# An expert's fixed number of rows: 608 instead of 640

## The chip, the cores and the metric

The kernel runs on one core of one Trainium2 chip. The metric is the device time of one execution in microseconds (us); three runs of the kernel before gave 948.78, 949.24 and 949.30, median 949.24. The engines: PE is TensorE's matmul, PEld its weight load, DVE VectorE, ACT ScalarE, POOL GpSimd (which also issues the indirect DMAs), SP SyncE (which issues the plain DMAs).

## The reference, cut to what matters

Attention within chunks of 64 gives 2304 tokens of 512 numbers; a dense layer with 2048 hidden units follows; then each token goes to two of eight experts, and the experts' weighted results are added up:

```python
def _moe2_ref(x, w_gate, w_noise, noise, w1, w2):     # x: 2304 x 512, after the dense layer
    logits = x @ w_gate
    noise_scale = np.log1p(np.exp(x @ w_noise))
    noisy_logits = logits + noise_scale * noise
    top2 = np.argpartition(-noisy_logits, 2, axis=1)[:, :2]
    ...                                               # top2_w: softmax over the two
    for e in range(E):                                # 8 experts
        for k in range(2):
            mask = top2[:, k] == e
            h = np.maximum(x[mask] @ w1[e], 0.0)      # 512 -> 1024
            out[mask] += top2_w[mask, k, None] * (h @ w2[e])   # 1024 -> 512
```

With two experts for each of 2304 tokens an expert has 576 rows on average. How many it really has is known on the chip only.

## The kernel before, in words

**Numbers.** Every f32 operand of the large products is split into a high part, rounded to the matmul's short f32 form (float32r), and a low part, the rest. A product is then three MATMULs (`PASSES`): high by high, high by low, low by high. The small products (attention, gate) are left in plain f32.

**Stages.** Five blocks of 4, 3, 4, 4 and 3 tiles of 128 tokens go through attention and the dense layer; the gate's results of each block are turned into places in a table in DRAM (`gate_ps`): each expert has a region of 2688 rows, and a token's row number and weight are scattered to the next free place of its two experts. Then come nine groups (`groups`): expert 0 in two parts (its first three tiles, and the two tiles up to `CAP`), experts 1 to 6 whole with five tiles each, and expert 7 again in two parts of three and two tiles. A part or an expert takes the first `CAP` = 640 places of its region, whether filled or not; unfilled places point at rows of zeros in DRAM. If an expert has more than `CAP` rows, `overflow` handles the rest after everything else.

**A group.** `exp_slots` or `exp_slots_q` fetches the places (`tab`, and for the second form `tq`, from which `exp_index` makes indices). The rows are fetched by indirect DMAs from GpSimd: `exp_gather` one per tile of 128 rows (for the second part of expert 0 and for expert 1), `exp_gather_q` four per tile, each for 32 rows cut into quarters (for all others). They are transposed on TensorE (`exp_tr`) or, the quarters, on VectorE (`exp_tr_q`, `quarters_t`), and ScalarE and VectorE write the high and the low part into Xa or Xe (Xb for the first group), which the groups use in turn.

Then the group runs over 8 units (`U2`) of 128 hidden numbers each. For a unit, `exp_h` makes the first products (L284): per half of the rows, 12 MATMULs (4 pieces of the 512 by 3 passes) with the unit's weights stationary and the rows as moving columns; with 640 rows that is two halves of 320, with 256 or 384 rows one of that width. ScalarE (L585) and VectorE (L586) take the result out of PSUM as the unit's high and low g. One unit later `exp_o` makes the second products (L293): for each tile, three MATMULs with the tile's 128 columns of g stationary and 512 columns of weights moving, all 8 units added up in PSUM. `exp_y` scales each tile's sum by the rows' weights (L612, L614; the very last tile in two halves, L609 and L610) and adds it to the output with an indirect DMA from GpSimd (L615).

**Order.** The order of work on TensorE, VectorE and ScalarE is written out by hand (`manual_schedule`); the loop at the end of `tile_kernel` puts the next group's gathers and transposes and the weights' splitting (`pump`: L128, L129) behind each unit. GpSimd's and SP's queues are ordered by a planner from its own estimates. A group's rows are asked for one group ahead: the first three tiles in units 3, 5 and 6 of the group before the last, the others early in the group before.

Of the kernel before, what the change touches and what calls it, by code (L numbers as in the profile page):

```python
# [8 lines left out]
F32 = mybir.dt.float32  # L9
# [4 lines left out]
AF = mybir.ActivationFunctionType  # L14
ALU = mybir.AluOpType
# [4 lines left out]
P = 128  # L20
NT = 2304
DM = 512
KD = DM // P
# [6 lines left out]
XO = [("a", 0), ("b", 0), ("a", 0), ("b", 0), ("a", 0)]  # L30
NB = len(BT)
GRP = list(zip(B0, BT))
CAP = 640
CT = CAP // P
EARLY = 384
RB = 21
RGN = RB * P
# [5 lines left out]
def tile_kernel(ctx, tc, qkv, w1u, w2u, wg, noise, out):  # L43
    nc = tc.nc
# [43 lines left out]
    cnt = const.tile([P, NE + 1], I32, name="cnt")  # L88
# [4 lines left out]
    arena = const.tile([P, 7, DM], F32, name="arena")  # L93
    X = {"a": const.tile([P, 8 * CAP], F32R, name="Xa")}
    late = tc.tile_pool(name="late", bufs=1)
# [4 lines left out]
    def xview(where, n):  # L100
        a, off = where
        return X[a][:, off:off + 8 * n].rearrange("p (j k n) -> p j k n", j=2, k=KD)

    xb = [xview(XO[b], BT[b] * P) for b in range(NB)]
    st = {}
# [183 lines left out]

    def s2(acc, g, w, tiles, first, last):  # L290
        for i in range(tiles):
            for j, (a, b) in enumerate(PASSES):
                nc.tensor.matmul(acc[i], g[:, a, i * P:(i + 1) * P], w[:, b, DM:],  # L293
                                 start=(first and j == 0), stop=(last and j == 2))
            tick()

# [7 lines left out]
    def gtile():  # L304
        return work.tile([P, 2 * CAP], F32R, tag="g", bufs=2, name="g")

# [49 lines left out]

    def quarters_t(dst, src):
        nc.vector.transpose(dst.rearrange("p (c b j) -> p c b j", c=KD, b=KD),  # L360
                            src.rearrange("p (c i b) -> p c b i", c=KD, b=KD))

    def gate_l(t):
        st.pop(("x2", t))
# [151 lines left out]
    def exp_slots(key, e, t0, nt, off):  # L516
        tab = work.tile([P, CT, 2], I32, tag="tab", bufs=4, name="tab")
        r0 = e * RGN + t0 * P
        nc.sync.dma_start(tab[:, :nt], table[r0:r0 + nt * P, :].rearrange("(t p) c -> p t c", p=P))
        st["tab", key] = tab  # L520
        st["xg", key] = xview(off, nt * P)


    def exp_slots_q(key, e, t0, nt, off):
# [14 lines left out]

    def exp_gather_q(key, i):  # L540
        xr = work.tile([P, DM], F32, tag="x2", bufs=3, name="xrq")
        for c in range(KD):
            nc.gpsimd.indirect_dma_start(  # L543
                out=xr[:, c * P:(c + 1) * P], out_offset=None, in_=x2q,
                in_offset=bass.IndirectOffsetOnAxis(ap=st["iq", key][:, i * KD + c:i * KD + c + 1], axis=0))
        st["xr", key, i] = xr

    def exp_tr_q(key, i):
        x = st["xg", key]
        xt = arena[:, 5 + i % 2]  # L550
        quarters_t(xt, st.pop(("xr", key, i)))
        xt = xt.rearrange("p (c b j) -> p b c j", c=KD, b=KD)
        hi, lo = (x[:, j, :, i * P:(i + 1) * P].rearrange("p b (c j) -> p b c j", c=KD) for j in range(2))
        nc.scalar.activation(hi, xt, AF.Copy)
        nc.vector.tensor_tensor(lo, xt, hi.bitcast(F32), op=ALU.subtract)

# [7 lines left out]
    def exp_tr(key, i):  # L564
        xr = st.pop(("xr", key, i))
        x = st["xg", key]
        pt = bank(("p7", "p6")[i % 2], [P, KD, P], "ptg")
        for kd, xc in enumerate(blocks_of(xr)):
            nc.tensor.transpose(pt[:, kd, :], xc, ident)  # L569
        hi, lo = (x[:, j, :, i * P:(i + 1) * P] for j in range(2))  # L570
        nc.scalar.activation(hi, pt, AF.Copy)
        nc.vector.tensor_tensor(lo, pt, hi.bitcast(F32), op=ALU.subtract)

    def exp_h(key, e, u, nt):
        x, w = st["xg", key], st["w", e, u]
        g = gtile()[:, :2 * nt * P].rearrange("p (j n) -> p j n", j=2)
        st["g", key, u] = g
        if nt * P <= 512:
            parts = [(0, nt * P)]
        else:  # L580
            parts = [(0, nt * P // 2), (nt * P // 2, nt * P // 2)]
        for t0, n in parts:
            h = hbank(n)
            s1(h, w, x, t0, n)
            nc.scalar.activation(g[:, 0, t0:t0 + n], h, AF.Relu)  # L585
            nc.vector.scalar_tensor_tensor(g[:, 1, t0:t0 + n], h, 0.0, g[:, 0, t0:t0 + n].bitcast(F32),  # L586
                                           op0=ALU.max, op1=ALU.subtract)

    def exp_last(key, e, nt):
        for i in range(nt):  # L590
            for u in (U2 - 2, U2 - 1):
                g, w = st["g", key, u], st["w", e, u]
                for j, (a, b) in enumerate(PASSES):
                    nc.tensor.matmul(st["acc", key][i], g[:, a, i * P:(i + 1) * P], w[:, b, DM:],  # L594
                                     start=False, stop=(u == U2 - 1 and j == 2))

    def exp_o(key, e, u, nt):
# [3 lines left out]

    def exp_y(key, e, nt):
        tab = st.pop(("tab", key))
        for i in range(nt):
            y = arena[:, i]
            sc = tab[:, i, 1:2].bitcast(F32)
            if key == (NE - 1, 1) and i == nt - 1:
                h = DM // 2
                nc.vector.tensor_scalar(y[:, :h], st["acc", key][i][:, :h], sc, None, op0=ALU.mult)  # L609
                nc.scalar.activation(y[:, h:], st["acc", key][i][:, h:], AF.Copy, scale=sc)  # L610
            elif i % 2 == 0:
                nc.vector.tensor_scalar(y, st["acc", key][i], sc, None, op0=ALU.mult)  # L612
            else:
                nc.scalar.activation(y, st["acc", key][i], AF.Copy, scale=sc)  # L614
            s = nc.gpsimd.indirect_dma_start(  # L615
                out=out, out_offset=bass.IndirectOffsetOnAxis(ap=tab[:, i, 0:1], axis=0),
                in_=y, in_offset=None, compute_op=ALU.add)
            for o in st.setdefault(("out_st", e), []):
                tc.declare_no_dep(s.ins, o.ins, reason="an expert has a token once")
            st["out_st", e].append(s)  # L620
# [11 lines left out]

    def overflow():
        for e in range(NE):
            n = nc.values_load(cnt[0:1, e:e + 1], min_val=0, max_val=RGN)
            with tc.For_i(CAP, n, P) as i:
                tab = work.tile([P, CT, 2], I32, tag="tab", bufs=4, name="tabo")
                nc.sync.dma_start(tab[:, 0], table[bass.ds(i + e * RGN, P), :])
                xr = work.tile([P, DM], F32, tag="x2", bufs=3, name="xo")
                nc.gpsimd.indirect_dma_start(out=xr, out_offset=None, in_=x2d,  # L640
                                             in_offset=bass.IndirectOffsetOnAxis(ap=tab[:, 0, 0:1], axis=0))
                pt = bank("p7", [P, KD, P], "pto")
                for kd, xc in enumerate(blocks_of(xr)):
                    nc.tensor.transpose(pt[:, kd, :], xc, ident)
                xt = arena[:, 5].rearrange("p (h k) -> p h k", h=KD)
                nc.scalar.activation(xt, pt, AF.Copy)
                acc = bank("p0", [P, DM], "acco")
                for u in range(U2):
                    raw = work.tile([P, 2 * DM], F32, tag="raw", bufs=3, name="rawo")
                    nc.sync.dma_start(raw, w2u[e * U2 + u])  # L650
                    h = bank(HB[u % 2], [P, P], "ho")
                    for kd in range(KD):
                        nc.tensor.matmul(h, raw[:, kd * P:(kd + 1) * P], xt[:, kd], start=(kd == 0), stop=(kd == KD - 1))
                    g = work.tile([P, DM], F32, tag="r", bufs=2, name="go")
# [4 lines left out]
                    out=out, out_offset=bass.IndirectOffsetOnAxis(ap=tab[:, 0, 0:1], axis=0),  # L659
# [289 lines left out]
    for i in range(3):  # L949
        at(side, EU + i, exp_tr, (0, 0), i)  # L950
# [131 lines left out]
```

## Time and profile before

| what | value |
|---|---|
| median of three runs | 949.24 us |
| span of the profiled execution | 947.0 us (the page shows no time of its own beyond the span) |
| PE busy | 921.0 us, 97% |
| DVE, ACT, POOL busy | 489.1, 336.3, 242.0 us |
| granted TensorE clock | 0.996 on the mean |
| first products with 320 columns (L284) | 576 on Xe, 576 on Xa |
| first products with 256 columns | 192 |
| quarter gathers (L543) | 120 |
| scatters to the output (L615) | 40 |

Matmuls are pipelined: the duration shown for one (310 ns for 320 columns) begins while the one before still runs, so the time that one product costs is read from the distance between starts, or from the chain of waits, which counts each only from the end of the one before. The granted clock is a share of 2.4 GHz.

### The profile page before, as it was taken

The numbers are of one execution on the slowest core, as the hardware profiler recorded it, in microseconds if no ns is written. First come the engines' busy times: TensorE is split into PE (matmuls) and PEld (weight loads), VectorE is DVE, ScalarE is ACT, GpSimd is POOL, SyncE is SP. The second block draws the span as 40 slices with busy tenths as digits, with TensorE's granted clock in tenths as the row PEclk, the third lists the DMA queues.
The fourth block names the chain that finished last, engine by engine and source line by source line (L and its number), as shares of the span: only waits on it lengthen the run. The fifth ranks groups of instructions, "written<-read, shape, count | busy, mean of one in ns | idle before, by whom it ended". The sixth has DMA issues, their size and how long they took to land. (4 is left out here: it accounts for less than half of the span.)

```text
span 947.0 us, 14446 instructions
## 1 busy us (share of the span) xinstructions
PE 921.0 (97%) x5814; PEld 780.9 (82%) x5814; DVE 489.1 (52%) x912; ACT 336.3 (36%) x644; POOL 242.0 (26%) x219
## 2 busy tenths in 40 slices
PE   6999999999999999999999999999999999999995
PEld 3677788887777777888988899989899899898894
DVE  7999954544453444456642555445545544441311
ACT  4555433332233222245531533333333333321210
POOL 0000000030002000213105166745736454432311
PEclk9999999999999999999999999999999999999998
DMA  9636549122112410025533663644636354140421
GB/s 342 207 99 204 175 146 343 35 68 68 34 34 57 134 35 1 1 90 91 188 101 67 169 155 107 146 119 101 143 113 143 115 122 129 51 59 20 56 33 27
DMA packets 50364, 102.41 MB, mean 108 GB/s; under 512 B 17136, under 2 KB 23152, under 8 KB 50288
## 3 DMA queue, kind: packets, MB, share of 16 engines
q1 hardware_dynamic: 38736, 80.38, 27.3%
q0 software_dynamic: 11552, 21.02, 12.0%
q8 instruction: 47, 0.77, 0.3%
q14 instruction: 29, 0.24, 0.1%
HBM read 78.05 MB, written 23.28 MB: 107 GB/s over the span
## 5 line engine op out<-in xcount | busy, mean ns | idle before, releaser
L293 PE MATMUL bp<-w,g 128*128 128x512 f32 x1812 | 455.1, 397 | 0.4 <-ACT g L320 0.3
L293 PEld LDWEIGHTS bp<-w,g 128*128 128x128 f32 x1812 | 333.5, 188 | 71.7 <-DVE g L325 0.8
L284 PE MATMUL bp<-Xa,w 128*128 128x320 f32 (+3 forms) x1344 | 248.5, 335 | 1.1 <-ACT w L168 0.9
L284 PEld LDWEIGHTS bp<-Xa,w 128*128 128x128 f32 x1344 | 214.9, 188 | 24.6 <-DVE w L175 2.1
L543 POOL DMA_INDIRECT xrq<-x2d,iq x120 | 129.9, 1082 | 97.3 <-DVE arena L360 33.1
L586 DVE SCALAR_TENSOR_TENSOR g<-bp,g 128x320 fp32r<-128x320 f32 (+2 forms) x128 | 62.8, 491 | 138.3 <-ACT g L585 138.3
L129 DVE TENSOR_TENSOR w<-raw,w 128x1024 fp32r<-128x1024 f32 x64 | 78.4, 1225 | 85.7 <-ACT w L128 85.7
L508 POOL DMA_INDIRECT table<-pay,slot x36 | 36.3, 1009 | 337.6 <-DVE slot L505 246.6
L585 ACT ACTIVATE g<-bp 128x320 fp32r<-128x320 f32 (+2 forms) x128 | 56.1, 438 | 176.2 <-PE bp L284 176.2
L284 PE MATMUL bp<-Xe,w 128*128 128x320 f32 (+1 forms) x672 | 106.6, 313 | 0.0
L284 PE MATMUL bp<-Xb,w 128*128 128x384 f32 (+1 forms) x480 | 106.0, 366 | 0.0
L284 PEld LDWEIGHTS bp<-Xe,w 128*128 128x128 f32 x672 | 103.4, 188 | 2.8
L319 DVE SCALAR_TENSOR_TENSOR r<-r,bp 128x512 f32<-128x512 f32 (+1 forms) x80 | 50.6, 633 | 91.7 <-ACT r L318 91.5
L284 PEld LDWEIGHTS bp<-Xb,w 128*128 128x128 f32 x480 | 85.3, 188 | 12.6 <-issue 1.8
L615 POOL DMA_INDIRECT out_dram<-arena,tab x40 | 63.1, 1576 | 122.2 <-DVE arena L612 98.8
L318 ACT ACTIVATE r<-bp,b 128x512 f32<-128x512 f32 (+1 forms) x80 | 51.3, 642 | 106.4 <-PE bp L284 106.4
L128 ACT ACTIVATE w<-raw 128x1024 fp32r<-128x1024 f32 x64 | 67.7, 1058 | 56.5 <-PE bp L293 56.5
L325 DVE TENSOR_TENSOR g<-r,g 128x512 fp32r<-128x512 f32 (+1 forms) x80 | 51.0, 637 | 40.2 <-ACT g L320 40.2
L320 ACT ACTIVATE g<-r 128x512 fp32r<-128x512 f32 (+1 forms) x80 | 47.1, 589 | 60.3 <-DVE r L319 60.3
L360 DVE STREAM_TRANSPOSE arena<-xrq 128x512 f32<-128x512 f32 x30 | 32.9, 1098 | 0.1
L168 ACT ACTIVATE w<-u 128x512 fp32r<-128x512 f32 x32 | 20.2, 633 | 32.5 <-DVE u L161 32.5
L727 POOL MEMSET zero<- 128x1024 f32 x1 | 1.0, 957 | 114.7 <-DVE u L161 114.7
(150 smaller groups left out, 485.2 us busy)
## 6 DMA issues: line engine op xcount, KB each, us to landing
raw<-in_w2u_dram SPq DMA_DIRECT2D x64, 512.0 KB, 3.9
raw<-in_w1u_dram SPq DMA_DIRECT2D x24, 512.0 KB, 4.7
arena<-in_qkv_dram SPq DMA_DIRECT2D x14, 768.0 KB, 4.2
out_dram<-zero SPq DMA_DIRECT2D x4, 1536.0 KB, 19.2
rawx<-in_w1u_dram SPq DMA_DIRECT2D x8, 512.0 KB, 10.1
x2d<-x SPq DMA_DIRECT2D x15, 256.0 KB, 3.3
xq<-x2d SPq DMA_DIRECT2D x44, 64.0 KB, 3.4
xrq<-x2d,iq POOLq DMA_INDIRECT x120, 3.0
```

What stands on the lines that cost most here:

```text
L128: nc.scalar.activation(w[:, 0], raw, AF.Copy)
L129: nc.vector.tensor_tensor(w[:, 1], raw, w[:, 0].bitcast(F32), op=ALU.subtract)
L284: nc.tensor.matmul(dst, w[:, a, kd * P:(kd + 1) * P], x[:, b, kd, t0:t0 + n], start=(k == 0), stop=(k == 3 * KD - 1))
L293: nc.tensor.matmul(acc[i], g[:, a, i * P:(i + 1) * P], w[:, b, DM:], start=(first and j == 0), stop=(last and j == 2))
L318: nc.scalar.activation(r, st["h", b], AF.Relu, bias=b3)
L319: nc.vector.scalar_tensor_tensor(r, r, 6.0, st["h", b], op0=ALU.min, op1=ALU.mult)
L320: nc.scalar.activation(st["g", b, u][:, 0], r, AF.Copy)
L325: nc.vector.tensor_tensor(g[:, 1], st["r", b], g[:, 0].bitcast(F32), op=ALU.subtract)
L543: nc.gpsimd.indirect_dma_start(out=xr[:, c * P:(c + 1) * P], out_offset=None, in_=x2q, in_offset=bass.IndirectOffsetOnAxis(ap=st["iq", key ...
L585: nc.scalar.activation(g[:, 0, t0:t0 + n], h, AF.Relu)
L586: nc.vector.scalar_tensor_tensor(g[:, 1, t0:t0 + n], h, 0.0, g[:, 0, t0:t0 + n].bitcast(F32), op0=ALU.max, op1=ALU.subtract)
L615: s = nc.gpsimd.indirect_dma_start(out=out, out_offset=bass.IndirectOffsetOnAxis(ap=tab[:, i, 0:1], axis=0), in_=y, in_offset=None, comput ...
```

## The change

`CAP` goes from 640 to 608. The number of tiles of an expert stays five; the fifth has 96 rows. Two helpers give the number of rows of a part (`cols`: 608 for a whole expert, 224 instead of 256 for the second parts of experts 0 and 7) and the columns of a tile (`tile_of`). With them, the rows' buffers are 608 wide, the first products run over two halves of 304 or one part of 224, the fifth tile's second products have 96 stationary columns and write 96 partitions, its scaling and its scatter take 96 rows, and its gather in quarters takes three DMAs of 32 rows instead of four. `exp_gather` (128 rows) and the transposes on TensorE are as before; the splitting behind them takes 96 columns. The places are fetched as before (five times 128). The overflow loop starts at 608, with another bound for its counter.

```diff
--- before.py
+++ after.py
@@ -30,8 +30,18 @@
 XO = [("a", 0), ("b", 0), ("a", 0), ("b", 0), ("a", 0)]
 NB = len(BT)
 GRP = list(zip(B0, BT))
-CAP = 640
-CT = CAP // P
+CAP = 608
+CT = -(-CAP // P)
+
+
+def cols(t0, nt):
+    return min(CAP - t0 * P, nt * P)
+
+
+def tile_of(x, i):
+    return x[:, :, i * P:min((i + 1) * P, x.shape[2])]
+
+
 EARLY = 384
 RB = 21
 RGN = RB * P
@@ -289,8 +299,9 @@
 
     def s2(acc, g, w, tiles, first, last):
         for i in range(tiles):
+            gi = tile_of(g, i)
             for j, (a, b) in enumerate(PASSES):
-                nc.tensor.matmul(acc[i], g[:, a, i * P:(i + 1) * P], w[:, b, DM:],
+                nc.tensor.matmul(acc[i][:gi.shape[2]], gi[:, a], w[:, b, DM:],
                                  start=(first and j == 0), stop=(last and j == 2))
             tick()
 
@@ -356,9 +367,10 @@
 
 
 
-    def quarters_t(dst, src):
-        nc.vector.transpose(dst.rearrange("p (c b j) -> p c b j", c=KD, b=KD),
-                            src.rearrange("p (c i b) -> p c b i", c=KD, b=KD))
+    def quarters_t(dst, src, c=KD):
+        dst, src = dst[:, :c * P], src[:, :c * P]
+        nc.vector.transpose(dst.rearrange("p (c b j) -> p c b j", c=c, b=KD),
+                            src.rearrange("p (c i b) -> p c b i", c=c, b=KD))
 
     def gate_l(t):
         st.pop(("x2", t))
@@ -518,7 +530,7 @@
         r0 = e * RGN + t0 * P
         nc.sync.dma_start(tab[:, :nt], table[r0:r0 + nt * P, :].rearrange("(t p) c -> p t c", p=P))
         st["tab", key] = tab
-        st["xg", key] = xview(off, nt * P)
+        st["xg", key] = xview(off, cols(t0, nt))
 
 
     def exp_slots_q(key, e, t0, nt, off):
@@ -539,7 +551,7 @@
 
     def exp_gather_q(key, i):
         xr = work.tile([P, DM], F32, tag="x2", bufs=3, name="xrq")
-        for c in range(KD):
+        for c in range(min(P, st["xg", key].shape[3] - i * P) // 32):
             nc.gpsimd.indirect_dma_start(
                 out=xr[:, c * P:(c + 1) * P], out_offset=None, in_=x2q,
                 in_offset=bass.IndirectOffsetOnAxis(ap=st["iq", key][:, i * KD + c:i * KD + c + 1], axis=0))
@@ -548,9 +560,10 @@
     def exp_tr_q(key, i):
         x = st["xg", key]
         xt = arena[:, 5 + i % 2]
-        quarters_t(xt, st.pop(("xr", key, i)))
-        xt = xt.rearrange("p (c b j) -> p b c j", c=KD, b=KD)
-        hi, lo = (x[:, j, :, i * P:(i + 1) * P].rearrange("p b (c j) -> p b c j", c=KD) for j in range(2))
+        n = min(P, x.shape[3] - i * P)
+        quarters_t(xt, st.pop(("xr", key, i)), n // 32)
+        xt = xt[:, :KD * n].rearrange("p (c b j) -> p b c j", c=n // 32, b=KD)
+        hi, lo = (x[:, j, :, i * P:i * P + n].rearrange("p b (c j) -> p b c j", c=n // 32) for j in range(2))
         nc.scalar.activation(hi, xt, AF.Copy)
         nc.vector.tensor_tensor(lo, xt, hi.bitcast(F32), op=ALU.subtract)
 
@@ -567,18 +580,17 @@
         pt = bank(("p7", "p6")[i % 2], [P, KD, P], "ptg")
         for kd, xc in enumerate(blocks_of(xr)):
             nc.tensor.transpose(pt[:, kd, :], xc, ident)
-        hi, lo = (x[:, j, :, i * P:(i + 1) * P] for j in range(2))
-        nc.scalar.activation(hi, pt, AF.Copy)
-        nc.vector.tensor_tensor(lo, pt, hi.bitcast(F32), op=ALU.subtract)
+        n = min(P, x.shape[3] - i * P)
+        hi, lo = (x[:, j, :, i * P:i * P + n] for j in range(2))
+        nc.scalar.activation(hi, pt[:, :, :n], AF.Copy)
+        nc.vector.tensor_tensor(lo, pt[:, :, :n], hi.bitcast(F32), op=ALU.subtract)
 
     def exp_h(key, e, u, nt):
         x, w = st["xg", key], st["w", e, u]
-        g = gtile()[:, :2 * nt * P].rearrange("p (j n) -> p j n", j=2)
+        n = x.shape[3]
+        g = gtile()[:, :2 * n].rearrange("p (j n) -> p j n", j=2)
         st["g", key, u] = g
-        if nt * P <= 512:
-            parts = [(0, nt * P)]
-        else:
-            parts = [(0, nt * P // 2), (nt * P // 2, nt * P // 2)]
+        parts = [(0, n)] if n <= DM else [(0, n // 2), (n // 2, n // 2)]
         for t0, n in parts:
             h = hbank(n)
             s1(h, w, x, t0, n)
@@ -589,9 +601,9 @@
     def exp_last(key, e, nt):
         for i in range(nt):
             for u in (U2 - 2, U2 - 1):
-                g, w = st["g", key, u], st["w", e, u]
+                g, w = tile_of(st["g", key, u], i), st["w", e, u]
                 for j, (a, b) in enumerate(PASSES):
-                    nc.tensor.matmul(st["acc", key][i], g[:, a, i * P:(i + 1) * P], w[:, b, DM:],
+                    nc.tensor.matmul(st["acc", key][i][:g.shape[2]], g[:, a], w[:, b, DM:],
                                      start=False, stop=(u == U2 - 1 and j == 2))
 
     def exp_o(key, e, u, nt):
@@ -601,19 +613,21 @@
 
     def exp_y(key, e, nt):
         tab = st.pop(("tab", key))
+        rows = st["xg", key].shape[3]
         for i in range(nt):
-            y = arena[:, i]
-            sc = tab[:, i, 1:2].bitcast(F32)
+            n = min(P, rows - i * P)
+            y, acc = arena[:n, i], st["acc", key][i][:n]
+            sc = tab[:n, i, 1:2].bitcast(F32)
             if key == (NE - 1, 1) and i == nt - 1:
                 h = DM // 2
-                nc.vector.tensor_scalar(y[:, :h], st["acc", key][i][:, :h], sc, None, op0=ALU.mult)
-                nc.scalar.activation(y[:, h:], st["acc", key][i][:, h:], AF.Copy, scale=sc)
+                nc.vector.tensor_scalar(y[:, :h], acc[:, :h], sc, None, op0=ALU.mult)
+                nc.scalar.activation(y[:, h:], acc[:, h:], AF.Copy, scale=sc)
             elif i % 2 == 0:
-                nc.vector.tensor_scalar(y, st["acc", key][i], sc, None, op0=ALU.mult)
+                nc.vector.tensor_scalar(y, acc, sc, None, op0=ALU.mult)
             else:
-                nc.scalar.activation(y, st["acc", key][i], AF.Copy, scale=sc)
+                nc.scalar.activation(y, acc, AF.Copy, scale=sc)
             s = nc.gpsimd.indirect_dma_start(
-                out=out, out_offset=bass.IndirectOffsetOnAxis(ap=tab[:, i, 0:1], axis=0),
+                out=out, out_offset=bass.IndirectOffsetOnAxis(ap=tab[:n, i, 0:1], axis=0),
                 in_=y, in_offset=None, compute_op=ALU.add)
             for o in st.setdefault(("out_st", e), []):
                 tc.declare_no_dep(s.ins, o.ins, reason="an expert has a token once")
@@ -632,7 +646,7 @@
 
     def overflow():
         for e in range(NE):
-            n = nc.values_load(cnt[0:1, e:e + 1], min_val=0, max_val=RGN)
+            n = nc.values_load(cnt[0:1, e:e + 1], min_val=0, max_val=NT)
             with tc.For_i(CAP, n, P) as i:
                 tab = work.tile([P, CT, 2], I32, tag="tab", bufs=4, name="tabo")
                 nc.sync.dma_start(tab[:, 0], table[bass.ds(i + e * RGN, P), :])
```

## Rows read from the trace of the kernel before

**Rows 1.** The page's first section: the span, then an engine's busy time, share and instructions.

```profile
span 947.0 us, 14446 instructions
PE 921.0 (97%) x5814; PEld 780.9 (82%) x5814; DVE 489.1 (52%) x912; ACT 336.3 (36%) x644; POOL 242.0 (26%) x219
```

**Rows 2.** A table by stretch: length; busy PE, PEld, DVE, ACT, POOL (instructions); clock; DMA.

```profile
510.00:542.00 32.00, 29.14 (x183) 25.60 (x182) 16.35 (x26) 13.37 (x22) 10.58 (x9) 1.00 0.65 165
542.00:912.00 370.00, 370.00 (x2044) 334.30 (x2043) 168.92 (x235) 118.85 (x190) 180.42 (x152) 1.00 0.43 102
912.00:937.00 25.00, 24.71 (x154) 21.65 (x152) 5.80 (x12) 3.77 (x9) 5.27 (x4) 1.00 0.25 33
```

**Rows 3.** The chain of waits in order of time: start, time on the chain, what.

```profile
589.68 3.52 PE bp L284 x24
593.20 3.50 PE bp L293 x15
...
903.66 2.09 PE bp L284 x12
...
915.53 1.43 PE bp L284 x12
916.96 1.39 PE bp L293 x6
```

**Rows 4.** Groups by line and shape: busy time, mean ns of one, idle before.

```profile
L284 PE MATMUL bp<-Xe,w 128*128 128x320 f32 x576 | 88.5, 310 | 0.0
...
L284 PE MATMUL bp<-Xa,w 128*128 128x256 f32 x192 | 25.7, 284 | 0.0
```

**Rows 5.** Groups of weight loads by line and shape.

```profile
L284 PEld LDWEIGHTS bp<-Xe,w 128*128 128x128 f32 x672 | 103.4, 188 | 2.8
...
L187 PEld LDWEIGHTS pair<-arena 64*64 64x64 f32 x448 | 7.8, 134 | 5.6 <-issue 3.7 <-DVE Xb L267 1.2 <-DMA xq<-x2d 0.4
...
L569 PEld LDWEIGHTS bp<-ident,xr 128*128 128x128 f32 x40 | 6.1, 205 | 4.4 <-DMA xr<-x2d,tab 2.3 <-issue 1.5
```

**Rows 6.** Timeline of PE, 510 to 533 us, and one line of L569's own view.

```profile
512.28 0.75 PE L569 MATMUL bp<-ident,xr 128*128 128x128 f32 x4 [1.32 <-DMA xr<-x2d,tab]
...
527.11 0.63 PE L569 MATMUL bp<-ident,xr 128*128 128x128 f32 x4
...
532.04 0.72 PE L569 MATMUL bp<-ident,xr 128*128 128x128 f32 x4 [1.46 <-DVE cnt L630]
...
L569 PE MATMUL bp<-ident,xr x40: 270/283/388, 456.9 to 542.4; 128*128 128x128 f32 x40
```

**Rows 7.** Timeline of DVE and of PE around the start of an expert.

```profile
644.99 0.69 DVE L555 TENSOR_TENSOR Xe<-arena,Xe 128x512 fp32r<-128x512 f32 x1 [0.70 <-ACT Xe L554]
...
652.62 3.69 PE L284 MATMUL bp<-Xe,w 128*128 128x320 f32 x24
```

**Rows 8.** GpSimd's last scatter; scatters' landing (L615's view); gathers (xrq's view).

```profile
938.25 1.55 POOL L615 DMA_INDIRECT out_dram<-arena,tab  x1 [0.30 <-issue]
...
DMA to landing us min/median/max: 4.7/5.5/6.6
...
L543 POOL DMA_INDIRECT xrq<-x2d,iq x120: 939/945/1910, 550.2 to 858.3; - x120
```

**Rows 9.** Timeline of PE, 142.7 to 150 us, with changes of the array's form.

```profile
142.78 0.86 PE L284 MATMUL bp<-Xb,w 128*128 128x384 f32 x4
143.57 0.43 PE L401 MATMUL bp<-at,wg_sb 128*32 128x128 f32 x8
143.92 0.97 PE L284 MATMUL bp<-Xb,w 128*128 128x384 f32 x4
144.82 0.69 PE L254 MATMUL pair<-at,arena 64*64 64x64 f32 x32
...
149.16 0.86 PE L284 MATMUL bp<-Xb,w 128*128 128x384 f32 x4
149.86 0.27 PE L413 MATMUL bp<-ident,lp 128*128 128x128 f32 x1
```

## The prediction

> **What bounds the kernel now.** I read the page's first section, then a table by stretch, then the chain of waits, then the groups by line and shape, and last single stretches of the timeline.
>
> The reader is to see in the first section that TensorE is busy for 97% of the span [rows 1]. That is an average, so the stretches matter: from 542 to 912 us, where the five-tile experts 1 to 6 and the first three tiles of expert 7 run, TensorE is busy for all 370 us at a granted clock of 1.00 (the 2.4 GHz level), while VectorE, ScalarE and GpSimd are busy for 169, 119 and 180 [rows 2]. From 510 to 542 us (the second part of expert 0) TensorE lacks 2.9 us, from 912 to 937 us (the second part of expert 7) 0.3 us. The chain of waits says the same: it is nothing but first products (L284) and second products (L293) in turn [rows 3]. So a first product that gets shorter moves everything behind it, and work taken from other engines is worth nothing here.
>
> The chain also gives the price of one product, which the groups don't: their mean of 310 ns for a 320-column product [rows 4] includes the pipeline, in which the next one has already started. From the chain, 24 products of 320 columns take 3.52 us, 146.7 ns each; 12 of 384 take 2.09 us, 174.2 ns; 12 of 256 take 1.43 us, 119.2 ns; 6 second products of 512 take 1.39 us, 232 ns [rows 3]. From 256 to 384 columns these lie on one line: 27.5 ns for each 64 columns, 0.43 ns a column, and some 9 ns that don't depend on the width.
>
> The sum is made against the profiled execution, whose span is 947.0 us [rows 1]; its own total isn't shown beyond the span. The median of the three runs is 949.24 us, 2.2 us more, which lie around the span; I take them over unchanged.
>
> **The change part by part.**
>
> *First products of the five-tile experts.* Two halves of 304 columns instead of 320. There are 576 of them on Xe [rows 4] and as many on Xa: 6 experts by 8 units by 24. On the line one of 304 takes 146.7 - 16 x 0.43 = 139.8 ns, 6.9 ns less; 1152 x 6.9 = 7.9 us. Both neighbours (256 and 320) are measured, so this is interpolation. The bounds: 0, if the engine takes columns in blocks larger than 16, which no row excludes, and 8.2 us with the slope from 320 to 512 columns, (232 - 146.7)/192 = 0.444 ns. I take 7.9. All of it lies on the path, since TensorE has no gap there [rows 2]. A unit should fall from 7.02 to 6.85 us, a group from 56.1 to 54.9.
>
> *First products of the two second parts* (expert 0 and expert 7). One product of 224 columns instead of 256; 192 of them [rows 4]. This is extrapolation: no first product in the trace is narrower than 256. By the line it would be 105.5 ns, 13.7 less, 2.6 us in all. Against it stand two kinds of rows. The weight load takes 188 ns for 128 columns and 134 for 64 [rows 5], so 54 ns for 64 columns, 0.84 ns a column, and 108 ns for the 128 themselves: about the 224-column product, which then no longer hides it. And a transpose with only 128 columns (L569) still starts about 117 ns after the one before: four take 0.63 us of which the last one's own 0.28 goes off, (0.63 - 0.28)/3 [rows 6], but its weights are read with a stride, and their load takes 205 ns instead of 188 [rows 5]. So the ends are 119 ns (no gain) and 105.5 (2.6 us); I take 110, nearest to the load of the unstrided weights, 9 ns less, 1.8 us. These stretches aren't free of waits: in the first, 1.46 us behind the counts (DVE cnt) and 1.32 us behind a gather come at fixed points in TensorE's order [rows 6], and neither depends on the width, so the saving passes them.
>
> The Trainium skill, page "TensorE: Matmul & The Clock Gate", section "Back-to-back issue gap", gives an isolated matmul N/2.4 + 2.5 ns: 109.2 ns for 256 columns and 95.8 for 224, so an estimate by that page is 13.3 ns x 192 = 2.6 us here instead of 1.8. The trace has 119.2 ns for 256, 10 ns above the rule, and the measured line is used.
>
> *Second products.* The fifth tile has 96 stationary columns instead of 128, but 512 moving columns as before, so their 232 ns stand. Their load (188 ns, by 0.84 ns a column some 161 for 96) is hidden behind the product ahead either way. Zero; if the narrower form broke the cover, it is the third case below.
>
> *Gathers.* The fifth tile of experts 2 to 6, and the last of expert 7, issue three quarter gathers instead of four: six fewer of 120, each 0.95 us on GpSimd by the median [rows 8]. Some 6 us of GpSimd, zero on the path: GpSimd is idle for half of the stretch [rows 2], and the last tile of the next expert is ready early: its low part (L555) is written by 645.68 us, the first product that reads it starts at 652.62 [rows 7], 6.9 us later. This slack is also the cover for anything that comes later on that queue because of the edit; a slip below it costs nothing, beyond it one for one.
>
> *Evictions, transposes, splits.* The two evictions of a unit get 16 columns of 320 shorter, the split of the fifth tile a quarter: off the path, since both engines are idle for more than half of the stretch [rows 2] and the 3.50 us of second products stand between a half's eviction and its use [rows 3]. Zero. TensorE's transposes for expert 0 and 1 stay at 128 columns and the gathers behind them (L559) at 128 rows.
>
> *Scatter.* Forty scatters stay, eight with 96 rows. Seven are covered by the next group's products. The last ends the kernel: issued at 938.25, 1.55 us on GpSimd, and the span ends 7.2 us after that; median landing 5.5 us [rows 8]. If a quarter of the rows took a quarter of both away it would be 1.8 us; if issue and landing are fixed, nothing. A gather with as many places and a fourth of the bytes still takes 0.95 us of GpSimd, so the bytes alone don't set it; I take 0.4.
>
> The sum: 7.9 + 1.8 + 0.4 = 10.1 us; 949.2 - 10.1 = **939.1 us**. By the ends, with the line's price for the wide part: 949.2 - 7.4 = 941.8 (short products and scatter give nothing and half a microsecond goes in shifted waits) to 949.2 - 12.6 = 936.6 (8.2 + 2.6 + 1.8).
>
> **The rivals.**
>
> *Narrow products fall off the line upwards* (slower). Place: the 192 products of 224 columns. The kernel has a form that is much dearer by column: its plain f32 products (L401) take two MATMULs each, and four of them side by side, with 128 columns, hold TensorE for 0.35 us (143.57 to 143.92) [rows 9]. With the 0.11 us for leaving that form (below) taken out it is 0.24 us, 1.9 ns a column, against 0.43. At that pace one of 224 takes 0.42 us, 0.30 more than now; x 192 = 58 us, less the 8.3 of the other two terms: 949.2 + 49.7 = **999 us**. The ends: two instructions at the 110 ns of a load, 0.10 more, 19 us, 960; the 0.35 unreduced, 0.61, 94 us, 1035. It turns the sign from 43 ns more on each (8.3 us/192). For it: not one row shows a rounded f32 product below 256 columns. Against: at 256 nothing bends yet, and the products of these groups are of the one-instruction form at every width. 14%.
>
> *The 96-column form makes the array switch* (about nothing, or slightly slower). Place: the fifth tile's second products, once in each of 8 units in 8 groups, in and out. Price: four products ahead of the 32-column form take 0.79 us (142.78 to 143.57) against 0.70 ahead of a 128-column one (149.16 to 149.86): 0.09 us to enter; four that come behind one switch and ahead of another take 0.90 (143.92 to 144.82): 0.11 to leave [rows 9]. 64 x 0.20 = 12.8 us, so 939.1 + 12.8 = **952 us**. For it: the trace does charge for changes of form. Against: the rows that pay are 64 and 32 columns wide, 96 doesn't fit either. 6%. The Trainium skill, page "TensorEngine Tiling (Array Packing)", section "Key Properties", says that a change of the tiling mode drains the engine; it lists widths of 32, 64 and 128 only, and no row here shows 96.
>
> *The gain is eaten by waits* (half or none left). Other engines lose time at a unit of 6.85 us, or the planner puts GpSimd's and SP's transfers in another order, and more than 6.9 us of slack go. Each group saves 1.3 us; with half lost, **944 us**, with all, 949. For it: those two queues aren't ordered by hand. Against: GpSimd idle for half of the stretch. 8%.
>
> *It doesn't do what it says*: an expert with more than 608 rows would enter the overflow loop. The reference on its own inputs gives 538 to 596 rows an expert, so no; 1%.
>
> **How the numbers follow.** The forecast has 71%, with a range of its own of 936.6 to 941.8. Faster by over 0.2% (about what a measurement of this kernel tells from no change, 1.9 us) is the forecast and a part of the eaten gain: 0.75. Within 0.2%: the rest of that and a cheap switch, 0.06. Slower: the dear narrow product and most of the switch, 0.19. The range of 936.5 to 952 holds the forecast, the eaten gain and the switch; the dear narrow product stays outside.
>
> **What would show it.** First products of 304 columns at 139.8 ns (24 in 3.36 us) and 12 of 224 in 1.32 us between second products; units of 6.85 us; no gap of TensorE from 542 to some 930 us; second products of a five-tile unit still 3.50 us for 15. Wrong would be: 12 products of 224 columns in more than 1.43 us, the fifth tile's second products starting more than 232 ns apart, or TensorE waiting at a group's start for Xa or Xe.

## The result and the profile after

The changed kernel takes 937.99 us (median of 4 runs, 937.46 to 938.20), the kernel before 949.27 (4 runs). The medians lie 11.3 us apart (ratio 0.9881); the ratio on record is 0.9875, with a 95% interval of 0.9862 to 0.9887. Forecast were 10.1 us, a ratio of 0.9894, just outside the interval. One of the twelve runs of second_only (below) took 3511.66 us, at a granted clock of 0.252 where the others had 0.988 to 0.996, and is left out of its ratio. Line numbers after the change are ten to fourteen higher: first products are L294, second products L304, the scatter L629.

The first section of the page after, beside [rows 1]:

```profile
span 936.1 us, 14441 instructions
PE 910.3 (97%) x5814; PEld 766.9 (82%) x5814; DVE 482.3 (52%) x912; ACT 333.3 (36%) x644; POOL 231.4 (25%) x213
```

The table by stretch (length; busy PE, PEld, DVE, ACT, POOL with instructions; clock; DMA), beside [rows 2]: TensorE is still busy for all of its stretch from 542 us on, at a granted clock of 1.00 (the 2.4 GHz level). VectorE and GpSimd are busy for a slightly smaller share of it than before (45% and 47% instead of 46% and 49%), ScalarE for 32% as before.

```profile
542.00:902.50 360.50, 360.50 (x2042) 322.28 (x2041) 162.65 (x235) 116.70 (x190) 169.16 (x146) 1.00 0.43 102
902.50:926.60 24.10, 24.10 (x154) 20.53 (x153) 5.31 (x11) 3.55 (x9) 4.90 (x4) 1.00 0.26 34
```

The chain of waits (start, time on the chain, what), beside [rows 3]. The reader is to see 24 first products of 304 columns in 3.36 us, as forecast (140.0 ns each), 12 of 224 in 1.33 (111 ns; 110 forecast), and two things that were not. A unit's 15 second products are quicker: the lines show 3.46 us against the 3.50 of [rows 3], but in the kernel before units of 3.50 and of 3.48 us take turns, so the means count: 3.472 us instead of 3.492 over experts 2 to 6, 0.02 us less. And 6 second products behind the narrow first products take 1.41 us instead of 1.39.

```profile
656.45 3.36 PE bp L294 x24
659.81 3.46 PE bp L304 x15
663.27 3.36 PE bp L294 x24
...
907.50 1.39 PE bp L304 x6
908.89 1.33 PE bp L294 x12
910.22 1.41 PE bp L304 x6
```

The other kind of unit in the kernel before:

```profile
600.22 3.48 PE bp L293 x15
```

The groups by line and shape (busy us, mean ns of one, idle before), beside [rows 4] and [rows 5]: 186 of the fifth tile's 192 second products have the form 128*96 here (the last six, of expert 7, stand under another line), and their weight load takes 161 ns, the number worked out from the loads of 64 and 128 columns.

```profile
L294 PE MATMUL bp<-Xe,w 128*128 128x304 f32 x576 | 84.7, 303 | 0.0
...
L304 PE MATMUL bp<-w,g 128*96 128x512 f32 x186 | 52.8, 392 | 0.0
...
L304 PEld LDWEIGHTS bp<-w,g 128*96 128x96 f32 x186 | 30.0, 161 | 11.1
...
L294 PE MATMUL bp<-Xa,w 128*128 128x224 f32 x192 | 24.1, 276 | 0.0
```

The timeline of TensorE at the two waits of [rows 6], and of GpSimd's last scatter, beside [rows 8]. The wait behind the counts is nearly the same (1.51 us, before 1.46), the one behind the gather is 0.64 us longer; the scatter of 96 rows takes GpSimd 1.43 us instead of 1.55, and the span ends 7.8 us after its start instead of 8.8.

```profile
512.93 0.75 PE L582 MATMUL bp<-ident,xr 128*128 128x128 f32 x4 [1.96 <-DMA xr<-x2d,tab]
...
532.17 0.72 PE L582 MATMUL bp<-ident,xr 128*128 128x128 f32 x4 [1.51 <-DVE cnt L644]
...
928.25 1.43 POOL L629 DMA_INDIRECT out_dram<-arena,tab  x1 [0.30 <-issue]
```

From the starts of the groups on TensorE the 10.99 us that the span lost come apart like this (us; the last matmul counts from its start):

| stretch | before | after | change |
|---|---|---|---|
| up to the first product of expert 0's second part | 517.20 | 517.73 | +0.53 |
| that part, up to expert 1 | 25.22 | 24.53 | -0.69 |
| experts 1 to 6 | 334.62 | 325.54 | -9.08 |
| first part of expert 7 | 34.80 | 34.77 | -0.03 |
| its second part, up to the last matmul | 24.49 | 23.75 | -0.74 |
| the end behind it | 10.72 | 9.74 | -0.98 |

### The profile page after: what moved, and what is told of

Same layout as the page of the kernel before. It is cut to its first block, busy times and chain, and to the rows that moved or that the text cites. A ratio compares the mean times of both kernels' runs of the same rounds, so it can differ in the third digit from the quotient of the medians.

```text
span 936.1 us, 14441 instructions
## 1 busy us (share of the span) xinstructions
PE 910.3 (97%) x5814; PEld 766.9 (82%) x5814; DVE 482.3 (52%) x912; ACT 333.3 (36%) x644; POOL 231.4 (25%) x213
## 5 line engine op out<-in xcount | busy, mean ns | idle before, releaser
L304 PE MATMUL bp<-w,g 128*128 128x512 f32 (+1 forms) x1812 | 454.2, 396 | 0.4 <-ACT g L331 0.3
L304 PEld LDWEIGHTS bp<-w,g 128*128 128x128 f32 (+1 forms) x1812 | 328.7, 185 | 73.6 <-DVE g L336 0.8
L294 PE MATMUL bp<-Xa,w 128*128 128x304 f32 (+3 forms) x1344 | 242.8, 331 | 1.1 <-ACT w L178 0.9
L294 PEld LDWEIGHTS bp<-Xa,w 128*128 128x128 f32 x1344 | 209.7, 189 | 25.5 <-DVE w L185 2.1
L555 POOL DMA_INDIRECT xrq<-x2d,iq x114 | 118.9, 1043 | 96.3 <-DVE iq L549 35.0
L598 DVE SCALAR_TENSOR_TENSOR g<-bp,g 128x304 fp32r<-128x304 f32 (+2 forms) x128 | 60.4, 472 | 132.4 <-ACT g L597 132.4
L597 ACT ACTIVATE g<-bp 128x304 fp32r<-128x304 f32 (+2 forms) x128 | 54.2, 424 | 168.4 <-PE bp L294 168.3
L294 PE MATMUL bp<-Xb,w 128*128 128x384 f32 (+1 forms) x480 | 106.0, 366 | 0.0
L294 PE MATMUL bp<-Xe,w 128*128 128x304 f32 (+1 forms) x672 | 102.7, 308 | 0.0
L294 PEld LDWEIGHTS bp<-Xe,w 128*128 128x128 f32 x672 | 99.8, 188 | 3.3
L294 PEld LDWEIGHTS bp<-Xb,w 128*128 128x128 f32 x480 | 85.4, 188 | 12.5 <-issue 1.8
L629 POOL DMA_INDIRECT out_dram<-arena,tab x40 | 62.7, 1566 | 124.3 <-DVE arena L626 101.4
L372 DVE STREAM_TRANSPOSE arena<-xrq 128x512 f32<-128x512 f32 (+1 forms) x30 | 31.4, 1045 | 0.1
```

The costliest lines, as they stand in the source:

```text
L294: nc.tensor.matmul(dst, w[:, a, kd * P:(kd + 1) * P], x[:, b, kd, t0:t0 + n], start=(k == 0), stop=(k == 3 * KD - 1))
L304: nc.tensor.matmul(acc[i][:gi.shape[2]], gi[:, a], w[:, b, DM:], start=(first and j == 0), stop=(last and j == 2))
L555: nc.gpsimd.indirect_dma_start(out=xr[:, c * P:(c + 1) * P], out_offset=None, in_=x2q, in_offset=bass.IndirectOffsetOnAxis(ap=st["iq", key ...
L629: s = nc.gpsimd.indirect_dma_start(out=out, out_offset=bass.IndirectOffsetOnAxis(ap=tab[:n, i, 0:1], axis=0), in_=y, in_offset=None, compu ...
```

## Experiments

They are all made from the changed kernel. My theory: the gain is the columns of the first products, at 0.43 ns each down to the width at which the weight load (an estimate of 108 ns, from [rows 5]) no longer hides, and all of it is on the path. Open after the result were three things: who gives the 0.02 to 0.03 us a unit in the second products, whether the last scatter's 1.0 us belongs to the change, and whether the longer wait of 0.64 us does.

**One half of the change each.** Two runs: only experts 1 to 6 with 608 places, and only the second parts with 224.

```diff
# five_only
-    return min(CAP - t0 * P, nt * P)
+    return nt * P if nt == 2 else min(CAP - t0 * P, nt * P)
# second_only (and the buffers X, g kept at 640 columns)
-    return min(CAP - t0 * P, nt * P)
+    return nt * P if nt == 5 else min(CAP - t0 * P, nt * P)
```

> Experts 1 to 6 have 608 places, the second parts of experts 0 and 7 keep 256. My theory (the change is worth what the first products lose in columns, 6.9 ns on each of 1152, and besides 27 to 33 ns on the 15 second products of a five-tile unit, because three of them load 96 columns instead of 128): 949.3 - 7.9 - 1.4 = 940.0 us; 24 products of 304 columns in 3.36 us, 15 second products in 3.47. Rival A (the second products' 0.03 us a unit has nothing to do with the 96 columns): 941.4. Rival B (most of the gain is the shorter end and the second parts): above 944.

> Experts 1 to 6 keep 640 places, only the second parts of experts 0 and 7 have 224. My theory: 192 products at 111 ns instead of 119.2 give 1.6 us, the 96-row scatter at the end 1.0: 949.3 - 2.6 = 946.7 us, and with the run before (five_only) the whole change adds up to 11.3. Rival (the longer wait at the first gather of expert 0, 1.96 us instead of 1.32, belongs to the narrower second part): 947.4, with that wait at about 2.0 here and at 1.3 in five_only; if the wait is jitter of the transfers it follows neither.

Measured: five_only 948.61 us against 957.89 before on the same chip, ratio 0.9897 (0.9878 to 0.9915): 9.3 us between the medians, 9.9 by the ratio; second_only 957.49, ratio 0.9991 (0.9977 to 1.0004): 0.4 us between the medians, 0.9 by the ratio. On this chip every kernel is slower than at first, before as well as after. The traces of the variants show a reason: a wait in the first five-tile expert that the first result's trace doesn't have; of the kernel before there is no trace from this chip. So what follows is read from stretches, and times go against the kernel before of the same chip alone. The chain of waits of five_only, and GpSimd's last scatter:

```profile
659.82 3.36 PE bp L294 x24
663.18 3.46 PE bp L304 x15
...
919.28 1.43 PE bp L294 x12
920.71 1.39 PE bp L304 x6
...
939.18 1.55 POOL L629 DMA_INDIRECT out_dram<-arena,tab  x1 [0.30 <-issue]
```

The same of second_only:

```profile
659.85 3.52 PE bp L294 x24
663.38 3.50 PE bp L304 x15
...
927.96 1.33 PE bp L294 x12
929.29 1.41 PE bp L304 x6
...
944.57 1.43 POOL L629 DMA_INDIRECT out_dram<-arena,tab  x1 [0.30 <-issue]
```

The gain sits where it was put: 24 products of 304 columns in 3.36 us in the one, the old 3.52 in the other; 12 narrow ones in 1.33 us in the other, the old 1.43 in the one. Expert 0's second part is 25.22 us long in five_only, to the digit as before, and 24.54 in second_only. But second_only fell short of its 2.6 us: its two stretches lose 1.4, which its interval (2.2 us faster to 0.4 slower) holds. The last line shows where the missing 1.0 us was: its last scatter has 96 rows, takes 1.43 us, and the span of 953.5 ends 8.9 us after its start; with 128 rows in five_only it is 947.2 - 939.18 = 8.0. So the end's 1.0 us doesn't follow the rows. And the wait behind the gather is 1.31 us in five_only and 1.18 in second_only, 1.96 in the changed kernel: it follows neither half.

**The fifth tile's second products and scatter at 128 again.**

```diff
# s2_full (g 640 columns per part)
+        full = nt * P
-        g = gtile()[:, :2 * n].rearrange("p (j n) -> p j n", j=2)
+        g = gtile()[:, :2 * full].rearrange("p (j n) -> p j n", j=2)
         ...
+        if full > n:
+            nc.vector.memset(g[:, :, n:full].bitcast(F32), 0.0)
# s2_scatter_full: besides
-        rows = st["xg", key].shape[3]
+        rows = nt * P
```

> The changed kernel, but the fifth tile's second products have all 128 stationary columns again (the 32 past the rows are set to zero by VectorE, one small memset a unit). My theory: the second products of a five-tile unit go back from 3.47 to 3.50 us, 48 x 0.03 = 1.4 us: 939.4. Rival A (their pace depends on the first products around them or on the run): 3.47 stays, 938.0. Rival B (the 96-column form makes the array switch and costs, hidden in the sum): 3.45 or less, below 937.5.

> As the run before (s2_full), and the fifth tile is scaled and scattered with all 128 rows. My theory: the end behind the last scatter's issue goes back from 7.81 to 8.8 us: 1.0 us more than s2_full, 940.4. Rival (the end's 1.0 us is the landing's own spread, 4.7 to 6.6 us in the trace of before): as s2_full, with the end anywhere between.

Measured: 947.68 us (ratio 0.9894, 0.9877 to 0.9912) and 948.15 (0.9898, 0.9874 to 0.9922): the whole times can't tell them apart. The chain of s2_full:

```profile
658.56 3.36 PE bp L294 x24
661.92 3.48 PE bp L304 x15
665.41 3.36 PE bp L294 x24
```

A unit (from one group of 24 to the next) takes 6.85 us against 6.82 in the changed kernel. Five groups, from expert 2 to the end of expert 6, take 273.86 us here, 272.90 in the changed kernel and 280.50 before: so of the 1.52 us that a group lost, the first products hold 1.33 and the second products 0.19. Times six that is 8.0 and 1.15. (This run also moves the low part of g; after_g640 below leaves it in this place and takes 96 columns.) The scatter: the span ends 8.3 us after the last scatter's start with 128 rows and 7.9 without, inside the spread of 7.7 to 8.9 that runs with 96 rows have among themselves. Only the 0.12 us on GpSimd are shown to be the change's; three ends with 128 rows (8.0, 8.3 and 8.8) are too few to tell a few tenths more.

**Other widths.** The changed kernel again beside one that uses 600 places, and two with 576 and 544 places, which leave out the rows that an expert has beyond them.

```diff
# cap600: products, scaling and scatter only; overflow from 600
+USED = 600
 ...
-        n = x.shape[3]
+        n = min(x.shape[3], USED - 3 * P if key[1] else USED) if nt in (2, 5) else x.shape[3]
# cap576 (cap544 likewise); overflow from 640
-CAP = 608
+CAP = 576
```

> The changed kernel once more, on the chip of the three runs beside it. All theories: 1.2% below the kernel before, as at first (0.9875).

> The changed kernel with first products, second products, scaling and scatter cut to the first 600 places of an expert (halves of 300, second parts of 216, a fifth tile of 88 rows); gathers, transposes and splits stay at 96 rows, and overflow begins at 600. My theory (0.43 ns a column down to 256 columns, the weight load's 108 to 111 ns below): 24 products in 3.32 us instead of 3.36, 1152 x 1.7 ns = 2.0 us, second parts nothing, 88 stationary columns 0.3 us: 2.3 us below the changed kernel. Rival A (the engine takes columns in blocks of 16, 304 being 19 of them): 3.36 us stays, as the changed kernel to 0.4 us. Rival B (a half that doesn't begin on a multiple of 64 bytes costs more): above the changed kernel.

> 576 places: halves of 288, second parts of 192, a fifth tile of 64 rows; what an expert has past 576 rows is left out. My theory: 24 first products in 3.19 us (132.9 ns); 12 of 192 columns in 1.30 to 1.33 us (108 to 111 ns, the weight load, not the line's 92); a fifth tile's second products at 226.5 ns (234 for 128 stationary columns, 230.5 for 96). Rival A (the array switches for the 64-column form): second products of a five-tile unit in 3.55 us or more instead of 3.45. Rival B (products under 256 columns get a slower pace the narrower they are): 12 of 192 in more than 1.33 us. Rival C (no load bound, the line goes on): 1.10 us.

> 544 places: halves of 272, second parts of 160, a fifth tile of 32 rows; the rest is left out. My theory: 24 first products in 3.03 us (126 ns), 12 of 160 columns in 1.30 to 1.33 us as for 192 and 224, a fifth tile's second products at 222.5 ns, 15 of a unit in 3.43 us. Rival A (switch for the 32-column form): 3.6 us or more. Rival C (line): 12 in 0.93 us.

Measured: after_again 945.78 us against 959.01, ratio 0.9874 (0.9847 to 0.9901), as at first. cap600 945.70, ratio 0.9874 (0.9850 to 0.9898): no different as a whole. cap576 and cap544 took 943.25 and 925.42 in one run each, 17.8 us apart; 11.8 of these lie in experts 1 and 2 (114.5 us against 102.7), where some 3 are the columns' and the rest the wait described below, which cap544 hardly has. The chains, cap600, cap576 and cap544 in this order:

```profile
640.77 3.50 PE bp L305 x15
...
657.89 3.30 PE bp L295 x24
661.19 3.48 PE bp L305 x15
...
916.34 1.33 PE bp L295 x12
917.67 1.41 PE bp L305 x6
```

```profile
658.97 3.18 PE bp L294 x24
662.15 3.50 PE bp L304 x15
...
913.56 1.32 PE bp L294 x12
914.88 1.41 PE bp L304 x6
```

```profile
660.90 3.03 PE bp L294 x24
663.93 3.48 PE bp L304 x15
...
896.85 1.30 PE bp L294 x12
898.15 1.42 PE bp L304 x6
```

| columns of a first product | 304 | 300 | 288 | 272 | 256 | 224 | 216 | 192 | 160 |
|---|---|---|---|---|---|---|---|---|---|
| ns each, from the chains | 140.0 | 137.5 | 132.5 | 126.3 | 119.2 | 110.8 | 110.8 | 110 | 108 |

Down to 256 the line holds, also at 300, so the engine doesn't take columns in blocks of 16. Below 256 it goes flat at 108 to 111 ns: neither the line (92 ns at 192 columns) nor a slower pace. It isn't a floor under every product: 32 of the 64*64 form take 0.69 us [rows 9]. What fits is the load of 128 stationary columns, for which the estimate of 108 ns was worked out from [rows 5] and which the moving columns don't change. But no run gives narrow first products a narrower load, so this cause is argued, not shown. The Trainium skill, page "TensorE: Matmul & The Clock Gate", section "LDWEIGHTS (loading the stationary operand)", gives a load columns / 1.2, 106.7 ns for 128; the pitches agree to 5 ns, while the loads' own durations are longer (188 ns for 128 columns, 161 for 96). The array charges nothing for the 64- and 32-column forms either (3.50 and 3.48 us for a unit's second products, not 3.55 or 3.6). But my theory of the second products fell here: with fewer stationary columns they don't get quicker in order; on the mean of experts 2 to 6, 128, 96, 88, 64 and 32 columns give 3.49, 3.47, 3.49, 3.50 and 3.48 us. And cap600 gained 0.9 us over five groups against after_again (271.99 against 272.91), not 1.9, mostly because it lost the second products' gain (0.02 us in each of 40 units).

The wait that the first result's trace doesn't have, in the timeline of after_again:

```profile
570.22 1.67 PE L294 MATMUL bp<-Xe,w 128*128 128x304 f32 x10 [1.77 <-issue]
572.71 0.44 PE L294 MATMUL bp<-Xe,w 128*128 128x304 f32 x2 [0.83 <-issue]
575.83 2.96 PE L294 MATMUL bp<-Xe,w 128*128 128x304 f32 x12 [2.69 <-DVE g L598]
```

TensorE stands three times in the first five-tile expert: 1.77 and 0.83 us with nothing shown that it waits for, then 2.69 us with VectorE's g as the last to come. The group takes 60.1 us instead of 52.6. Not all of that is standing: TensorE is busy for 2.72 of the 8 us from 568 to 576, and behind them the granted clock is lower, 0.57 and 0.90, between the 1.2 and the 2.4 GHz level. There 12 first products take 2.76 us and 15 second products 4.03, instead of 1.68 and 3.47, some 1.6 of the 7.5 us. The table by stretch:

```profile
576.00:579.00 3.00, 3.00 (x13) 2.92 (x14) 2.05 (x3) 2.06 (x4) 1.63 (x2) 0.57 0.10 26
579.00:583.00 4.00, 4.00 (x18) 3.21 (x17) 3.11 (x5) 1.07 (x3) 1.20 (x2) 0.90 0.57 165
```

On the chip of the four runs above it is the same: 60.8 us with 320 columns (second_only), 61.2, 60.7 and 60.8 with 304 (five_only, s2_full, s2_scatter_full). The 1.5 us that this group gains on the first chip, from 54.1 to 52.6, are gone there. So the rival of a gain eaten by waits does occur, in that run, in one group of six. The chip alone doesn't make the wait, since cap544 on the chip of after_again stands for 0.24 us there. What is late I haven't tested.

**The second products' 0.02 to 0.03 us.** Where g lies had changed with the width too: its low part 608 or 544 columns behind the high one in the quicker kernels, 640, 600 or 576 in the others. Three runs are to take this apart, and one restores the fourth quarter gather.

```diff
# cap600_g608: cap600 with the parts of g 608 columns apart
# after_g640 (s2_full_g672 likewise, 672, with s2_full's 128 columns and memset)
-        return work.tile([P, 2 * CAP], F32R, tag="g", bufs=2, name="g")
+        return work.tile([P, 2 * 640], F32R, tag="g", bufs=2, name="g")
 ...
-        g = gtile()[:, :2 * n].rearrange("p (j n) -> p j n", j=2)
+        g = gtile().rearrange("p (j n) -> p j n", j=2)[:, :, :n]
# gather4
-        for c in range(min(P, st["xg", key].shape[3] - i * P) // 32):
+        for c in range(KD):
```

> The kernel with 600 used places, but the two parts of g lie 608 columns apart instead of 600 (in cap600 15 second products took 3.50 us, in the changed kernel 3.47). Theory D (the second products' pace is set by where the low part of g lies: 608 and 544 columns after the high part are 19 and 17 times 128 bytes, and gave 3.47; 640, 600 and 576 gave 3.50): 24 first products in 3.32, 15 second products in 3.47 us, a group 54.3 us, 1.9 us below the changed kernel in all. Rival E (the pace goes by the number of stationary columns, 96 and 32 being fast, 128, 88 and 64 slow): 3.50 us, as cap600.

> The changed kernel with the two parts of g 640 columns apart instead of 608, 96 stationary columns as they are. Theory D (place of the low part): 15 second products in 3.50 us. Rival E (number of stationary columns): 3.47 us.

> 128 stationary columns in the fifth tile's second products again, but the two parts of g 672 columns apart (21 times 128 bytes) instead of 640. Theory D (place): 15 second products in 3.47 us. Rival E (number of columns): 3.49 us as in s2_full. If both this and after_g640 go against D, it is the columns.

> The changed kernel, but the fifth tile's gathers take all four quarters again (120 quarter gathers, the fourth one's rows aren't used). My theory: nothing, groups of 54.6 us from the second five-tile expert on, GpSimd some 6 us busier. Rival (the last quarter gather of a tile was late for the transpose): a wait of TensorE at the start of some group, 1 us or more in all.

Measured on a chip on which the kernel before takes 949.25 us: cap600_g608 936.67, ratio 0.9863 (0.9847 to 0.9880); after_g640 939.08, s2_full_g672 939.44, gather4 939.91 in one run each. The chains of after_g640, s2_full_g672 and cap600_g608 in this order:

```profile
650.60 3.36 PE bp L294 x24
653.96 3.46 PE bp L304 x15
```

```profile
650.59 3.36 PE bp L294 x24
653.95 3.48 PE bp L304 x15
...
914.39 1.39 PE bp L304 x6
```

```profile
640.21 3.48 PE bp L305 x15
...
650.47 3.30 PE bp L295 x24
653.77 3.48 PE bp L305 x15
```

By these lines alone theory D would fall: with the parts 640 apart the 96-column form keeps its 3.46 us, and 672 apart the 128-column form doesn't reach it. But they are units on Xe; on Xa cap600 takes 3.50 us and cap600_g608 3.48. The means over all units of experts 2 to 6, from the start of a unit's first second product to that of the next first product:

| stationary columns of the fifth tile | parts of g apart | run | us for a unit's 15 |
|---|---|---|---|
| 128 | 640 | before, second_only | 3.492 |
| 128 | 640 | s2_full | 3.494 |
| 128 | 672 | s2_full_g672 | 3.485 |
| 96 | 608 | changed kernel | 3.472 |
| 96 | 640 | after_g640 | 3.473 |
| 88 | 600 | cap600 | 3.492 |
| 88 | 608 | cap600_g608 | 3.479 |
| 64 | 576 | cap576 | 3.500 |
| 32 | 544 | cap544 | 3.480 |

So neither theory holds alone, and both in part. With g in the same place (640) the step from 128 to 96 columns gives 0.02 us, and most of it sits in the fifth tile's own three products (681 ns in after_g640, 699 in s2_full). With the same columns the place gives 0.013 us (88 columns, 600 to 608), 0.009 (128, 640 to 672) or nothing (96, 608 to 640). Why stays open. cap600_g608 gains on the changed kernel by stretches (five groups 271.36 us against 272.90), but the interval of its ratio overlaps the changed kernel's: not shown to be faster as a whole.

GpSimd's quarter gathers in gather4 and the starts of two groups of TensorE:

```profile
L555 POOL DMA_INDIRECT xrq<-x2d,iq x120 | 127.5, 1063 | 89.6 <-issue 32.0 <-DVE arena L372 29.8 <-DVE iq L549 27.5
...
651.30 3.52 PE L294 MATMUL bp<-Xe,w 128*128 128x304 f32 x24
...
705.91 3.51 PE L294 MATMUL bp<-Xa,w 128*128 128x304 f32 x24
```

The six gathers come back (120, 8.6 us more of GpSimd than the 118.9 with 114), and a group takes 54.61 us as in the changed kernel: they were hidden.

## Why the prediction was right, step by step

*Bound.* Right: TensorE sets the end of every stretch from expert 0's second part on; in the profiled result nothing else moved it, and the gathers' six were worth nothing (gather4).

*First products of 304 columns.* Right: 7.9 us forecast, 8.0 measured (1.33 a group, with the second products held at 128 columns). The forecast group of 54.9 us is a slip in the sum (8 units of 6.85 are 54.8); 54.6 were measured, the rest being the second products.

*First products of 224 columns.* Right in mechanism, a little high in size: 110 ns forecast, 110.8 measured, but 1.43 us in the two stretches instead of 1.8. Sixteen units save 0.10 us each, and 0.02 come back in most of them: the six second products behind take 1.41 us instead of 1.39 (1.41 to 1.43 also behind 216, 192 and 160 columns). The narrow first products aren't enough for that, since with the parts of g 672 apart (s2_full_g672) the six take 1.39 again; it moves with the place of g, which the prediction didn't look at. That the load sets the pace was its reason for 110, and the flat pitches fit it. The 2.6 us by the Trainium skill's page "TensorE: Matmul & The Clock Gate", section "Back-to-back issue gap", were farther off than the 1.8.

*Second products.* Wrong as a term: "512 moving columns as before, so their 232 ns stand". They lost 0.02 us a unit, 1.0 to 1.15 us in all: 1.15 from s2_full, 1.1 with g in the same place (five groups of after_g640 in 272.96 us against 273.86). It is the columns and in part the place of g; why isn't settled.

*Scatter.* Too high in size as far as shown: 0.4 us forecast, 0.12 on GpSimd follow the rows. The rest of the profiled end's 0.98 can't be told from spread.

*Waits.* The wait behind the gather went from 1.32 to 1.96 us in the profiled run; 1.12 to 1.87 in the other runs, with any width. It doesn't follow the change.

So without spread the sum is 8.0 + 1.4 + 1.15 + 0.1 = 10.7 us against 10.1, and the profiled pair's 10.99 holds besides a longer wait of 0.5 us and a shorter end of 0.9. That the sum came this near is in part luck: the second products' 1.1 us, forecast as nothing, and 0.7 us too much in the second parts and the scatter offset each other in part. The mechanism, columns on a path that is all TensorE, gave the 8.0.

*The rivals.* A dear narrow product: refuted down to 160 columns. A switch of the array: refuted for 96, 88, 64 and 32 stationary columns (no unit's 15 second products above 3.50 us on the mean). A gain eaten by waits: not in the profiled result; on two other chips the 1.5 us of one group are gone in the traces. An overflow: no instruction of its loop stands in the trace after.

## What to carry to other kernels

Where TensorE is the bound over a whole stretch, a column less of the moving operand is worth its place on the line of pitches, read from the chain and not from the mean durations; the line ends here between 256 and 224 columns with 128 stationary ones, where the estimate of the weight load lies, and below that at most 3 ns more were had from narrowing down to 160. One profiled end or one wait for a transfer moves by 1 us between runs: a change in it is the change's only if it follows the edit in a second kernel.

## What was not expected of the hardware

In the changed kernel a second product starts 226 to 237 ns after the one before, in an order that repeats from unit to unit. The 15 of a unit take 3.472 to 3.500 us by kernel; both the stationary columns and the place of g move this, the columns not in order. GpSimd's last scatter isn't in order of its rows either: 1.55 us for 128, 1.43 for 96, 1.58 for 88 (cap600), 1.42 for 64 (cap576). The kernel before took 949.3 us beside the first result and beside the last four runs, and 957.9 and 959.0 on two other chips; in the traces that the changed kernel and its variants left on those two, most of the difference is a wait in one expert's stretch.
